# Pairing input rows to shorten the even-frequency DFT matmuls, and loading channel 128 in 16 rows in place of 8, in a fused FFT and cosine-gated layer kernel

## The chip, the cores and the metric

The kernel runs on one core of a Trainium2 chip. The metric is the time on the device in microseconds (us), as the median of several executions. The profile's "span" is the time from the first to the last instruction of one profiled execution; it is about 2 us shorter than the device time of the same execution.

A NeuronCore has several engines that run their own instruction streams and wait for each other through semaphores. In the profile they are called PE (matrix multiply, with PEld for its weight loads), DVE (vector), ACT (scalar and activation functions), POOL (a second elementwise engine, slower here: 1.00 us for a 128x381 add, where DVE takes 0.95 us for 128x762; it also issues gathers) and SP (here it only issues DMA transfers; "SPq" lines are these issues). In this kernel data from DRAM comes by DMA, and channel 128 is also moved across partitions by DMA.

## The reference, cut to what matters

```python
def _attn_ref(x):                       # x: (8, 3008, 256) float32
    X = np.fft.fft(x, axis=1)           # along the 3008 rows
    X = np.fft.fft(X, axis=2)           # along the 256 channels
    return X.real.astype(np.float32)

def _moe_ref(x, w_in, w_out):           # x: (24064, 256), w_in: 256 x 2048, w_out: 2048 x 256
    h = x @ w_in
    g = h * np.cos(h)
    return (g @ w_out).astype(np.float32)
```

The output is the second function applied to the first, with the batch and row axes merged. Everything is float32.

## The kernel before

The channel transform is multiplied into `w_in` once, at the start, so only the row transform (a DFT of length 3008) is left to do per batch. It is done as matmuls with constant cosine and sine matrices.

Symmetry keeps these small. Rows `s`, `1504-s`, `1504+s` and `3008-s` are first added and subtracted ("folds"), so only rows 0 to 752 are left as the contraction. Each batch then has four transforms: real and imaginary part, each for even and odd frequencies `k`. Even `k` has 377 output columns (`NE`) and odd `k` 376 (`NO`).

The 753 rows lie as 128 partitions by six "slots" `m`. In every transform the even rows contribute to columns `k` and their mirror alike, so their matmuls need only half the columns (four matmuls of `NH` = 189, the "first part", then unfolded by DVE). The odd rows fill three slots, which need all 377 columns each (the "second part"). In the kernel before:

```python
NH = 189

def _row_of(m):                       # slot m, partition p -> row
    p = np.arange(128)
    return 4 * p + m if m < 4 else 512 + 2 * p + m - 4

def dft_parts(ri, kodd, par):
    mats = MC[ri, kodd]
    if par:                           # second part: odd rows, slots 1, 3, 5
        n = NO if kodd else NE
        for t in range(3):
            c = AW + t * NE
            yield 2 * t + 1, 0, mats[:, c : c + n]
    else:                             # first part: even rows
        for t, m in enumerate((0, 4, 2, 4)):
            yield m, t // 2 * NH, mats[:, t * NH : (t + 1) * NH]
```

Rows are loaded by plain DMA where they ascend with the partition (`L[0]` and `L[3]`). The mirrored ones come by indirect DMA ("gather"), issued by POOL, since they descend: four gathers per batch.

```python
GATHERS = [(2, 0), (2, 1), (1, 0), (1, 1)]
...
eng = nc.gpsimd if b == 1 else nc.sync        # plain loads: batch 1 on POOL's queue
for j, row in ((0, 0), (3, HALF)):
    pin(eng.dma_start(out=L[j][:, 0 : 4 * ND], in_=xrows(b, row, 4, 128, 4)))
    pin(eng.dma_start(out=L[j][:, 4 * ND :], in_=xrows(b, row + 512, 2, 128, 2)))
```

Channel 128 is handled apart, because the 129 distinct channels don't fit on 128 partitions. `load_ext` picks that one channel out of `x` (4-byte elements, a whole row apart in DRAM). `turn_ext` stores it to DRAM (`xe_dr`) and reads it back with rows on partitions (`xs`). `fold_ext`, on POOL, folds it; `dft_ext`, on PE, transforms it.

```python
def turn_ext():
    rows, xs = state["rows"], state["xs"]
    for j in range(4):
        spin(out=xe_dr[j], in_=rows[j][:, 0:768])             # spin = DMA issued by SP
    for j in range(4):
        spin(out=xs[:, j, :, 0:4], in_=xe_dr[j][:, 0:512].rearrange("b (p m) -> p b m", m=4))
        spin(out=xs[:, j, :, 4:6], in_=xe_dr[j][:, 512:768].rearrange("b (p m) -> p b m", m=2))
```

All engines' work is placed in one static schedule. `at(t, fn)` places the emission of `fn` at a nominal time. It fixes the order of the instructions on each engine, not the time at which they run. One "step" (nominal `T` = 4.8 us) handles 256 columns of the result, and there are 376 steps.

```python
e0 = 12 * T
at(e0 + 1.35, fold_ext)                   # POOL
at(e0 + 4.75, dft_ext)                    # PE
...
for b in range(1, NB):
    s0 = (b - 1) * steps_b                # steps_b = 47
    l0 = s0 - (8 if b > 1 else 0.5)       # loads and gathers, from step l0
    f0 = max(7, s0 - 1)                   # folds on POOL, from step f0 to f1
    f1 = s0 + 38
    ...                                   # DFTs: even k at s0+28 and s0+34, odd k at s0+38 and s0+42
```

## Time and profile before

| | before |
|---|---|
| device time, median of 3 | 1956.05 us (1955.8 to 1957.27) |
| profiled span, mean granted PE clock | 1954.1 us, 0.999 |
| PE busy | 1936.6 us, 99% |
| one step (11 matmuls of 256 columns) | 4.75 us |

The first part of the page gives each engine's busy time, its share of the span and its count of instructions. The fourth part gives the shares of the chain of waits, followed back from the last instruction. The kernel before:

```profile
span 1954.1 us, 28165 instructions
PE 1936.6 (99%) x8858; PEld 1650.5 (84%) x8858; DVE 1418.9 (73%) x2354; ACT 1453.6 (74%) x2791; POOL 1357.7 (69%) x1869
...
PE 92%; DVE 3%; ACT 1%; issue 1%; POOL 1%; DVEq 0%; POOLq 0%
```

PE is the limit: it idles 17.5 us out of 1954. A change can win only by giving PE less to do, and it loses by making PE wait.

The timeline view has one line per run of equal instructions: start in us, duration in us, engine, source line, operation, output and inputs, shapes, count and, in brackets, idle time before it and what ended it. PE in one even transform of the kernel before, its first part and its second part:

```profile
182.53 1.45 PE L266 MATMUL H<-MC,e 128*128 128x189 f32 x8
...
193.32 2.07 PE L266 MATMUL H<-MC,e 128*128 128x377 f32 x6
```

(Each matmul instruction appears as two records.) The second line is what the change shortens. The two times include some overlap at the ends, so that group costs PE 1.9 us up to the next one (at 195.23 us).

The start, on DVE and PE; "e" is the even fold, "pA" the first DFT, "H<-Rr,Wc" the first matmul of the main loop's step 0:

```profile
18.75 0.17 DVE L352 COPY e<-xl 128x6 f32<-128x6 f32 x1
```

```profile
21.82 1.55 PE L266 MATMUL pA<-MC,e 128*128 128x189 f32 x8 [0.77 <-DVE e L331]
...
31.57 1.02 PE L266 MATMUL H<-Rr,Wc 128*128 128x256 f32 x4
```

And channel 128: the DMA issues on SP, then POOL's fold of it ("xs", "xe").

```profile
24.09 52.95 SPq L168 DMA_DIRECT2D x<-in_x_dram  x5
77.16 13.87 SPq L168 DMA_DIRECT2D xe_dr<-x  x4
91.08 6.32 SPq L168 DMA_DIRECT2D xs<-xe_dr  x8
```

```profile
98.96 1.00 POOL L331 TENSOR_TENSOR e<-xl 128x381 f32<-128x381 f32 x1
99.91 0.39 POOL L275 TENSOR_TENSOR xs<-xs 128x96 f32<-128x96 f32 x1
```

The loads occupy SP's queue for 53 us, and POOL reaches its fold at 99.91 us without a wait.

### The profile page before, as it was taken

To read this page: it belongs to the slowest core of one execution; us is meant where nothing else is said; L and a number is where in the kernel's file an instruction comes from. 1 tells how busy PE (TensorE), PEld (TensorE's weight loads), DVE (VectorE), ACT (ScalarE), POOL (GpSimd) and SP (SyncE) were. 2 spreads that over 40 slices of the span, in tenths; PEclk is the share of its full clock that TensorE was granted. 3 is DMA by queue.
4 is the path that set the end of the run, shared out by engine and by line. 5 is a ranking of instruction groups with operands and counts; after the bars stand their busy time and mean duration, and the time that the engine had idled before them with its cause. 6 is when DMAs were issued, how large, how long until landed. Compare 5 with 4: busy or idle time off the path is not lost.

```text
span 1954.1 us, 28165 instructions
## 1 busy us (share of the span) xinstructions
PE 1936.6 (99%) x8858; PEld 1650.5 (84%) x8858; DVE 1418.9 (73%) x2354; ACT 1453.6 (74%) x2791; POOL 1357.7 (69%) x1869
## 2 busy tenths in 40 slices
PE   9999999999999999999999999999999999999998
PEld 4878888888888888888888888888888888888887
DVE  5777677777777767777677777777767777677777
ACT  3777777777777777777777777777777777777775
POOL 5977667776677766777677776777657776555654
PEclk9999999999999999999999999999999999999999
DMA  9720210102111020110301003011030100000101
GB/s 301 6 39 9 65 33 20 26 9 68 28 20 21 9 83 17 21 20 9 87 19 18 16 9 87 11 27 20 9 82 12 30 19 10 14 11 15 19 12 22
DMA packets 260161, 66.16 MB, mean 34 GB/s; under 512 B 247283, under 2 KB 250107, under 8 KB 260012
## 3 DMA queue, kind: packets, MB, share of 16 engines
q1 hardware_dynamic: 253292, 49.93, 13.8%
q0 software_dynamic: 4544, 14.17, 2.3%
q8 instruction: 70, 1.15, 0.2%
q14 instruction: 79, 0.65, 0.1%
q10 hardware_dynamic: 2176, 0.26, 0.1%
HBM read 39.48 MB, written 24.79 MB: 33 GB/s over the span
## 4 chain that ended last, share of the span: by engine, by line
PE 92%; DVE 3%; ACT 1%; issue 1%; POOL 1%; DVEq 0%; POOLq 0%
PE H L266 37%; PE pB L266 16%; PE pC L266 16%; PE pD L266 16%; PE pA L266 8%; DVE G L723 1%; ACT G L278 1%; POOL G L275 1%; DVE v L272 0%; DVE G L272 0%; DVE M L272 0%; ACT E L278 0%; DVE ab L272 0%; DVE u L272 0%; DVE ot L831 0%
## 5 line engine op out<-in xcount | busy, mean ns | idle before, releaser
L275 POOL TENSOR_TENSOR G<-G 128x256 f32<-128x256 f32 x1500 | 1079.2, 730 | 560.0 <-DVE G L723 467.8
L723 DVE SCALAR_TENSOR_TENSOR G<-H,G 128x512 f32<-128x512 f32 x376 | 257.0, 684 | 266.4 <-ACT G L278 266.4
L272 DVE TENSOR_TENSOR G<-H,G 128x512 f32<-128x512 f32 x376 | 260.0, 692 | 220.8 <-ACT G L278 217.8
L278 ACT ACTIVATE G<-H 128x512 int32<-128x512 f32 x376 | 224.6, 597 | 233.3 <-DVE G L272 231.9
L266 PE MATMUL pC<-G,WT 128*128 128x256 f32 x1504 | 387.4, 379 | 2.3 <-DVE u L272 1.9
L266 PE MATMUL H<-Ir,Ws 127*128 127x256 f32 x1504 | 387.5, 379 | 0.7 <-ACT E L278 0.7
L266 PE MATMUL H<-Rr,Wc 128*128 128x256 f32 x1504 | 387.2, 380 | 1.0 <-ACT H L278 0.8
L278 ACT ACTIVATE H<-Rb,wex 128x256 f32<-128x256 f32 x752 | 360.2, 479 | 25.9 <-DVE G L723 10.7
L278 ACT ACTIVATE E<-H 128x512 f32<-128x512 f32 x376 | 224.3, 596 | 200.7 <-PE H L266 198.0
L266 PEld LDWEIGHTS H<-Rr,Wc 128*128 128x128 f32 x1504 | 283.6, 190 | 49.1 <-ACT H L278 3.3
L266 PEld LDWEIGHTS pC<-G,WT 128*128 128x128 f32 x1504 | 283.8, 189 | 46.5 <-PE H L266 6.4
L266 PEld LDWEIGHTS H<-Ir,Ws 127*128 127x128 f32 x1504 | 282.3, 189 | 45.0 <-ACT E L278 6.1
L278 ACT ACTIVATE G<-G,halfpi 128x512 f32<-128x512 f32 x376 | 269.5, 717 | 1.5 <-DVE G L272 1.5
L272 DVE TENSOR_TENSOR M<-G,M 128x512 f32<-128x512 f32 x376 | 257.7, 685 | 0.0
L272 DVE TENSOR_TENSOR G<-E,H 128x512 f32<-128x512 f32 x376 | 255.3, 679 | 1.8 <-issue 1.7
L723 DVE SCALAR_TENSOR_TENSOR G<-G,M 128x512 f32<-128x512 f32 x376 | 254.2, 676 | 0.4 <-ACT M L278 0.3
L278 ACT ACTIVATE M<-M,halfpi 128x512 f32<-128x512 f32 x376 | 246.4, 655 | 0.4 <-DVE M L272 0.3
L266 PE MATMUL pB<-G,WT 128*128 128x256 f32 x752 | 227.4, 384 | 1.0 <-POOL G L275 0.8
L278 ACT ACTIVATE M<-G 128x512 int32<-128x512 f32 x376 | 224.1, 596 | 0.0
L266 PE MATMUL pB<-G,w 128*128 128x256 f32 x752 | 223.7, 379 | 0.1
L266 PE MATMUL pA<-G,w 128*128 128x256 f32 x752 | 223.8, 379 | 0.0
L266 PE MATMUL pD<-G,WT 128*128 128x256 f32 x752 | 223.8, 379 | 0.0
(134 smaller groups left out, 1793.6 us busy)
## 6 DMA issues: line engine op xcount, KB each, us to landing
out_dram<-ot SPq DMA_DIRECT2D x496, 32.0 KB
xl<-in_x_dram SPq DMA_DIRECT2D x14, 512.0 KB
out_dram<-ot SPq DMA_DIRECT2D x256, 2.0 KB
MC<-dft_mats SPq DMA_DIRECT2D x4, 943.5 KB
Rb<-r SPq DMA_DIRECT2D x10, 376.0 KB
xl<-in_x_dram SPq DMA_DIRECT2D x14, 256.0 KB
w<-in_moe_w_in_dram SPq DMA_DIRECT2D x4, 512.0 KB
w<-in_moe_w_out_dram SPq DMA_DIRECT2D x1, 2048.0 KB
```

Source lines behind the costliest of these rows:

```text
L266: nc.tensor.matmul(out_, lhsT=lhsT, rhs=rhs, start=start, stop=stop, skip_group_check=True)
L272: pin(nc.vector.tensor_tensor(out=o, in0=a, in1=b, op=op))
L275: pin(nc.gpsimd.tensor_tensor(out=o, in0=a, in1=b, op=op))
L278: pin(nc.scalar.activation(out=o, in_=i, func=func, **kw))
L723: nc.vector.scalar_tensor_tensor(out=o, in0=h, scalar=TWO_PI, in1=c, op0=ALU.mult, op1=ALU.mult)
```

## The change

For even `k`, rows `s` and `752-s` have equal cosines and sines up to a sign that depends on the parity of `k/2`. If both lie on one partition, they can be summed and differenced first; half of the columns need only the sum, and half only the difference. So two slots of odd rows at 377 columns each become one sum at 189 columns and one difference at 188: three 377-column passes become two. The price is a new layout. Slot D1 holds rows `247-2p`, which descend with the partition, so more slots must be gathered (4 gathers per batch become 10). The even columns come out sorted by parity, so writes into the ring are strided and split in two. Channel 128 follows the same layout and is loaded with 16 (half, batch) rows outermost in place of 8 batches. The core of the diff:

```diff
-NH = 189
+NK = 189
+NH = (190, 189)
+C0, D1, C2, Y, M1, X1 = range(6)
 def _row_of(m):
-    return 4 * p + m if m < 4 else 512 + 2 * p + m - 4
+    return (4 * p, 247 - 2 * p, 4 * p + 2, 504 + 2 * p, 505 + 2 * p, 249 + 2 * p)[m]
 ...
-    GATHERS = [(2, 0), (2, 1), (1, 0), (1, 1)]
+    GATHERS = [(0, (D1, D1 + 1)), (3, (D1, D1 + 1))] + [
+        (j, part) for j in (2, 1) for part in ((5, 6), (3, 4), (1, 3), (0, 1))
+    ] + [(1, (4, 5))]                                   # the last one in the last batch only
 ...
-        eng = nc.gpsimd if b == 1 else nc.sync          # 4 plain loads per batch
+        pin(nc.sync.dma_start(out=out, in_=in_))        # 8 plain loads per batch, all on SP
 ...
+        def pair(key, s, width, first, second):         # sum -> pf, difference -> slot M1
+            d, m = (s[:, n * width : (n + 1) * width] for n in (D1, M1))
+            tt(pf[:, 0:width], d, m, first)
+            tt(m, d, m, second)
 ...
     def dft_parts(ri, kodd, par):
+        if kodd:
+            parts = ((D1, 0, NO), (X1, 0, NO), (M1, 0, NO))
+        else:
+            parts = ((6, 0, NK), (M1, NK, NE - NK), (X1, 0, NE))    # 6 = the sum tile pf
 ...
     def turn_ext():
-            for j in range(4):
-                spin(out=xe_dr[j], in_=rows[j][:, 0:768])
+            for g in range(2):
+                spin(out=xe_dr[g], in_=rows[g][:, 0:768])
+                spin(out=xr_dr[g], in_=rows[g][:, 247::-1])         # reversed, to DRAM
 ...
+                spin(
+                    out=xs[0:124, g, :, 7:8],
+                    in_=xr_dr[g].rearrange("b (p m) -> p b m", m=2)[:, :, 0:1],
+                )
 ...
-    fold_now("z1 z3 c0 e0 o0 c3 e3 c2 e2 E2 x1 c1 e1 E0 EO0")       # batch 0, on DVE
+    fold_now("z1 z3 c0 e0 o0 c3 e3 c2 e2 E2 x1 c1 e1 E0 EO0 P0")
-        l0 = s0 - (8 if b > 1 else 0.5)
+        l0 = s0 - (8 if b > 1 else 1.2)
```

`in_=rows[g][:, 247::-1]` is a store to DRAM that reads its source backwards, one float at a time.

## The prediction

> **What bounds it.** TensorE: the page gives PE 99% busy (1936.6 of 1954.1 us), the chain of waits is 92% PE, and PE's waits sum to about 10 us. A plain step (eleven 256-column matmuls) repeats every 4.75 us in the timeline; DVE, ACT and POOL work in its shadow. Clock 0.999.
>
> **What is removed.** In the timeline three 377-column matmuls take 1.90 us from first start to the next group: 1.68 ns a column (256 columns: 0.433 us). Even k now streams 189+188+377 = 754 columns instead of 1131, and 4x190 instead of 4x189: 373 columns, 0.62 us less per even transform. Batches 1 to 7: 14 x 0.62 = 8.7 us. The channel-128 transform: perhaps 0.2 us. Batch 0's three even transforms (1.9 us of PE) lie in the start, where PE waits for DVE; I count nothing there.
>
> **What is added.**
> 1. POOL: gathers per batch go from 4 to 10 (0.97 us each, about 1.1 us with issue). The sums take 3.03 us per 4.75 us step, a fold 1.0 (1.15 with its copy). A gather alone fits; gather plus fold (5.1 to 5.3 us) doesn't. By the instruction order they meet in three steps per batch (four in the last). Before, POOL's idle there after the fold is 0.2, 0.7, 0.6 us, so it falls about 1.7 us behind; the third sum is finished about 0.9 us before PE loads weights from it. Estimate: PE loses 0.8 us per batch from batch 2 on, about 4.5 us in all, as "PE pB <- POOL G". The pair sums (two of about 0.46 us) have steps of their own: free.
> 2. DVE/ACT: strided ring writes split each 377-column write in two (DVE 0.54 becomes about 0.68 us, ACT 0.48 about 0.65): free from batch 1 on.
> 3. Start: DVE is busy without a gap from 18.5 to 30 us and the first main matmul (31.6 us) waits for it. P0, P2, two tiny adds and split writes add about 1.2 us. Ten gathers at 1.27 us end at 15 us and land at 18 to 19, when the fold that needs the last of them ran (18.8). About 1.3 us lost.
> 4. Channel 128: 53 us of issue on SP (24,576 elements). The Trainium skill, "DMA: Bandwidth & Descriptors", section "Why a DMA increments its semaphore by 16 and not by 1", says a copy uses the largest count up to 16 that divides the slowest dimension: 8 before, 16 now. I expect about 27 us. Batch 1's loads follow on the same queue and arrive near 58 us, before folds at 75. But reversed copies add small elements, and 124 partitions give 4 engines; POOL's fold of it (at 100 us) may wait: 1 us expected, at most 5.
>
> **Sum.** -8.9 +4.5 +1.3 +1 = -2, and I lean to less POOL loss: **1952 us**, range 1945 to 1958. Faster by over 2%: 0.5%; within 2%: 98.5%; slower by over 2%: 1%.
>
> **What would show it.** PE busy down about 10 us. PE waits for POOL G at three steps per batch, total 3 to 6 us (before 0.8). First main matmul at 32 to 34 us. The SP issue of channel 128 about halved. POOL busy up about 55 us.
>
> **What would make it wrong.** POOL's slack larger (then 1946); the channel-128 fold or batch-1 loads late, stalling POOL for many us (1960); strided PSUM or SBUF access costing DVE much more.

## The result, and the profile after

| | before | after |
|---|---|---|
| device time, median of 4 runs each | 1956.36 us (1955.8 to 1957.27) | 1985.84 us (1984.26 to 1989.48) |
| ratio | | 1.0153 (95%: 1.0135 to 1.017) |
| profiled span, granted PE clock | 1954.1 us, 0.999 | 1982.3 us, 0.992 |

A ratio here is the mean time of one kernel's fast runs over that of the other's fast runs of the same rounds, so it is not quite the ratio of the medians. The changed kernel is 1.5% slower. That is within 2%, as the prediction's likeliest class had it, but 1985.84 us lies far outside its range of 1945 to 1958, and on the wrong side of zero.

The page of the changed kernel: its busy times, two rows of its 40-slice table (busy tenths of PE, then the granted clock in tenths), and the chain of waits.

```profile
span 1982.3 us, 28384 instructions
PE 1932.9 (98%) x8858; PEld 1649.2 (83%) x8858; DVE 1425.2 (72%) x2386; ACT 1454.8 (73%) x2807; POOL 1418.9 (72%) x1947
...
PE   7959999999999999999999999999999999999998
...
PEclk9979999999999999999999999999999999999999
...
PE 84%; DVE 5%; POOL 4%; ACT 3%; issue 2%; SPq 1%; DMA 1%; DVEq 0%; POOLq 0%
```

PE is busy less than before (1932.9 us against 1936.6), as the change wants. But PE idles 49 us in place of 17.5. The table says where: a slice is 49.6 us, and apart from the last slice, which ran out in the kernel before as well, PE is below 9 tenths only in the first and the third. In the third the granted clock also drops. The view of waits names the wait, as engine, tile, who is waited for, total us, number and longest:

```profile
PE H L276 <- POOL xe L285: 23.7, 1, 23.7
PE pA L276 <- DVE e L341: 2.6, 1, 2.6
PE pB L276 <- POOL G L285: 2.3, 8, 0.6
```

One wait of 23.7 us, for POOL's fold of channel 128, is most of the loss of 28. POOL itself was waiting, as its timeline shows:

```profile
104.17 1.00 POOL L341 TENSOR_TENSOR e<-xl 128x381 f32<-128x381 f32 x1
129.22 0.59 POOL L285 TENSOR_TENSOR xs<-xs 128x64 f32<-128x64 f32 x2 [24.05 <-DMA out_dram<-ot]
```

The bracket blames a DMA "out_dram<-ot", the store of results. That label is an inference from semaphore events, and the instruction doesn't read `ot`; it reads `xs`. The DMA records agree: the last 4-byte packet of the reads into `xs` ended at 128.95 us, 0.27 us before POOL went on. What SP was doing until then shows why. Its timeline in the changed kernel:

```profile
25.13 27.06 SPq L162 DMA_DIRECT2D x<-in_x_dram  x3
52.33 14.81 SPq L182 DMA_DIRECT2D xl<-in_x_dram  x8
67.20 0.42 SPq L162 DMA_DIRECT2D xe_dr<-x  x1
67.66 0.65 SPq L162 DMA_DIRECT2D xr_dr<-x  x1
68.36 6.57 SPq L162 DMA_DIRECT2D xe_dr<-x  x1
74.97 1.93 SPq L162 DMA_DIRECT2D xr_dr<-x  x1
77.01 39.34 SPq L162 DMA_DIRECT2D xs<-xe_dr  x3
```

The issue time of the loads was indeed halved, 52.95 us to 27.06, and the first store was issued 10 us earlier than before. Then the first three reads of `xs` take 39 us to issue, where all eight took 6.32 us before. They follow the two reversed stores to `xr_dr`.

PE did not simply lose those 24 us. It came back to a slow clock:

```profile
130.26 3.73 PE L276 MATMUL H<-MC,xe 128*8 128x190 f32 x28 [23.66 <-POOL xe L285]
```

In the kernel before, the same 28 records took 2.09 us:

```profile
101.32 2.09 PE L266 MATMUL H<-MC,xe 128*8 128x189 f32 x28
```

The wait of 23.7 us and these 1.6 us make 25.3 us together. In the view by windows (window and its length, busy us and instructions of PE, PEld, DVE, ACT and POOL, granted clock, DMA share, GB/s) the clock shows directly:

```profile
110.00:115.00 5.00, 0.00 (x0) 0.00 (x0) 0.00 (x0) 0.00 (x0) 0.00 (x0) 0.50 0.26 5
...
130.00:135.00 5.00, 4.74 (x33) 2.64 (x34) 0.00 (x0) 0.00 (x0) 4.63 (x9) 0.68 0.32 51
```

During the stall the granted clock was 0.50, and 0.68 in the window from 130 to 135 us, in which PE resumes. The clock records behind this view have it at 0.50 from 109.30 us, 2.7 us after PE's last matmul, to 133.19 us. The Trainium skill, "TensorE: Matmul & The Clock Gate", section "Why this matters for your kernels", asks for no PE idle gap above about 3 us, since such a gap brings the gate back to half rate. This trace agrees: a gap of 23.7 us, and a clock of 0.50.

### A ledger by steps

Every step of the main loop begins with the same matmul, "H<-Rr,Wc". Its start in one trace minus its start in the other, over the 376 steps, is a running account of who is ahead. From the two traces (us; a positive number means that the changed kernel is late):

```
step   what lies there                                change of the offset    offset
0      start of the main loop                            +4.30                  4.30
1-12   end of the start                                  +0.9                   5.21
13     channel-128 fold                                  +25.4                 30.58
17-29  folds of batch 1, on POOL                         +1.2                  31.75
s0+31, s0+37 in batches 1-7: 14 even transforms          -0.50 to -0.63 each, -8.6 in all
s0+2 to s0+4 in batches 2-7: gathers beside folds        +0.8 to +1.0 each, +5.2 in all
others (small steps)                                     +0.5
after step 319                                           -0.7
end                                                                            28.2
```

So the change did win what it was made for, 8.6 us. It lost 25.4 us once, 5.2 us at the start, and 6.4 us in POOL's gathers and folds.

The gain and its mechanism are visible in the transform. The first even transform of batch 1 in the changed kernel, its second part:

```profile
225.08 0.48 PE L276 MATMUL H<-MC,pf 128*128 128x189 f32 x2
225.40 1.12 PE L276 MATMUL H<-MC,e 128*128 128x188 f32 x4
```

The 128x189 pass on the sum ("pf") and the passes on the other two slots take the place of the six records of 377 columns above. (The second line groups the 188-column difference with the 377-column slot, under the first one's shape.) Up to the next matmul, at 226.35 us, they cost 1.27 us, where the old group cost 1.9.

At the start, DVE waits for a gather, and PE for DVE:

```profile
21.37 0.17 DVE L362 COPY e<-xl 128x6 f32<-128x6 f32 x1 [3.81 <-DMA xl<-in_x_dram,ix]
```

```profile
24.43 2.90 PE L276 MATMUL pA<-MC,e 128*128 128x190 f32 x8 [2.59 <-DVE e L341]
...
35.87 1.13 PE L276 MATMUL H<-Rr,Wc 128*128 128x256 f32 x4 [0.26 <-issue]
```

DVE gets to this copy 2.6 us later than before (18.75). From there to the end of the unfold that frees bank pA for PE's next transform it takes 11.3 us in place of 9.5, so it adds 1.9 us of work: the pair sums, the small sums for channel 128, and the split unfold. That transform is then 0.2 us shorter on PE, and 2.6 + 1.9 - 0.2 = 4.3 us is what step 0 is late. (The pA group also takes 2.90 us in place of 1.55, at a granted clock of 0.50, which lasted from 23.97 to 27.38 us. That costs nothing: PE is idle again later, for 1.55 us from 31.3 us, until DVE has freed pA at 32.7 us.)

### The profile page after: what moved, and what is told of

It is laid out like the page before. It is cut to its first block, busy times and chain, and to the rows that moved or that the text cites. A ratio compares the mean times of both kernels' runs of the same rounds, so it can differ in the third digit from the quotient of the medians.

```text
span 1982.3 us, 28384 instructions
## 1 busy us (share of the span) xinstructions
PE 1932.9 (98%) x8858; PEld 1649.2 (83%) x8858; DVE 1425.2 (72%) x2386; ACT 1454.8 (73%) x2807; POOL 1418.9 (72%) x1947
## 4 chain that ended last, share of the span: by engine, by line
PE 84%; DVE 5%; POOL 4%; ACT 3%; issue 2%; SPq 1%; DMA 1%; DVEq 0%; POOLq 0%
PE H L276 33%; PE pB L276 14%; PE pC L276 14%; PE pD L276 14%; PE pA L276 7%; POOL G L285 2%; DVE G L790 2%; ACT G L288 1%; SPq L162 1%; POOL xl L152 1%; DVE G L282 1%; POOL e L341 1%; DVE v L282 1%; DVE M L282 1%; ACT E L288 1%
## 5 line engine op out<-in xcount | busy, mean ns | idle before, releaser
L276 PE MATMUL pD<-G,w 128*128 128x256 f32 x752 | 223.7, 379 | 0.0
```

The source lines that it names most:

```text
L276: nc.tensor.matmul(out_, lhsT=lhsT, rhs=rhs, start=start, stop=stop, skip_group_check=True)
```

## The experiments

The main theory was that the reversed stores of channel 128 to DRAM (4-byte elements) drain so slowly that every later transfer of the chain is late. Its rivals were the new place of batch 1's loads, which now stand ahead of the channel-128 stores on SP's queue, and the two reads of 124 partitions (E3). All edits are against the changed kernel. "Jump" is what the offset to the kernel before gains between step 12 and step 13; in the changed kernel it is 25.4 us. E1 to E4 ran together on one chip, E5 to E7 on a second, E8 and E9 on a third.

### E1: reverse on ScalarE, store contiguously

```diff
-                spin(out=xr_dr[g], in_=rows[g][:, 247::-1])
+    def reverse_ext():
+        act(x1[0 : 4 * NB, 768:1016], x1[0 : 4 * NB, 247::-1])     # one ACT copy
+        for g in range(2):
+            spin(out=xr_dr[g], in_=rows[g][:, 768:1016])
+        ...                                                        # then the xs reads, as they were
+    at(7 * T + 1.46, reverse_ext)
```

> The change, but the reversal of channel 128's rows is done by one ScalarE copy in SBUF and the store to the scratch tensor is then a plain one of contiguous rows. Theory R (the reversed store, 7936 elements of 4 bytes, is the stall: it held the queue from about 71 to 109 us): the copies behind it end near 97 us, the channel-128 fold on POOL no longer waits 24 us, PE's 23.7 us wait vanishes, about 1960 us. Rival Q (batch 1's plain loads, moved to the SP queue ahead of it, are the delay): little change, 1980 us or more.

Measured: correct, 1960.04 us (1958.71 to 1961.37, 2 runs) against 1956.59 us before; ratio 1.0016 (0.9987 to 1.0045). The jump is 0.07 us, and the 23.7 us wait is gone. The reversal is one ACT instruction, and the reads that follow now issue without delay:

```profile
78.67 0.39 ACT L289 ACTIVATE x<-x 32x248 f32<-32x248 f32 x1
```

```profile
79.09 0.77 SPq L163 DMA_DIRECT2D xr_dr<-x  x2
79.97 2.99 SPq L163 DMA_DIRECT2D xs<-xe_dr  x3
```

A 0.39 us instruction in an idle spot of ACT buys back 25 us. The batch-1 loads and the 124-partition reads are still as in the changed kernel, so neither of them makes the stall by itself. Since E1 changes the element size as well as the timing of the chain, the next three runs hold the rivals against each other.

### E2: batch 1's plain loads back on POOL's queue

```diff
+        eng = nc.gpsimd if b == 1 else nc.sync
         def load(out, in_):
-            pin(nc.sync.dma_start(out=out, in_=in_))
+            pin(eng.dma_start(out=out, in_=in_))
```

> The change, but batch 1's eight plain loads are issued by POOL again, as before, so they don't stand ahead of channel 128's copies on the SP queue. Theory Q: the stall goes, about 1960 to 1965 us. Theory R: the copies only start some 6 us earlier, the stall shrinks from 24 to about 18 us, about 1980 us.

Measured: correct, 1987.98 us (1986.97 to 1988.99, 2 runs), ratio 1.0159 (1.0129 to 1.0188). The reads of `xs` hang just as long, and PE's wait stays:

```profile
77.26 40.10 SPq L162 DMA_DIRECT2D xs<-xe_dr  x3
```

```profile
PE H L278 <- POOL xe L287: 20.6, 1, 20.6
```

The jump is 23.0 us, and it is smaller only because PE arrives 4.7 us later: POOL's fold starts at 130.89 us, 1.7 us later than in the changed kernel (129.22). Without the loads ahead of them, the reversed stores were issued no earlier (69.27 and 75.87 us, against 67.66 and 74.97), so the order of SP's queue is not the cause. The move even costs 4.6 us elsewhere, between steps 1 and 6: POOL spends the time until 50.2 us on issuing gathers and these eight loads, and PE then waits 3.6 us for its sums. That the change moved these loads to SP was right.

### E3: the 124-partition reads in two pieces, 112 and 12

```diff
-                spin(
-                    out=xs[0:124, g, :, 7:8],
-                    in_=xr_dr[g].rearrange("b (p m) -> p b m", m=2)[:, :, 0:1],
-                )
+                for p0, p1 in ((0, 112), (112, 124)):
+                    spin(
+                        out=xs[p0:p1, g, :, 7:8],
+                        in_=xr_dr[g].rearrange("b (p m) -> p b m", m=2)[p0:p1, :, 0:1],
+                    )
```

> The change, but the two 124-partition copies of channel 128 are cut into 112 + 12 partitions[...]. If the 4-engine copies carry the stall (theory F): about 1962 us. Theory R: they are two times 6 us of a chain of 60, so 8 to 10 us of the stall go, about 1976 us.

Measured: correct, 1983.54 us (1982.88 to 1984.2, 2 runs), ratio 1.0136 (1.0107 to 1.0166). The jump is 21.6 us, against 25.4:

```profile
PE H L276 <- POOL xe L285: 19.6, 1, 19.6
```

The 8 to 10 us that were expected did not come: the jump is 3.8 us smaller. Part of that is the start of this run, which was 1.5 us later, so that PE had less to wait. POOL's fold starts 2.5 us earlier than in the changed kernel (126.67 us against 129.22), though the first read of `xs` moved 2.3 us later (105.64 against 103.35). The 124-partition reads are thus a small part, some 2 to 5 us; one trace of each doesn't settle it closer, since the time from the first read to the fold also differs among runs with unsplit reads (25.9 us in the changed kernel, 23.4 in E8). The Trainium skill, "DMA: Bandwidth & Descriptors", section "Why a DMA increments its semaphore by 16 and not by 1", says that the number of engines is the largest one up to 16 that divides the slowest dimension of both sides. That gives 4 engines for 124 partitions, and 16 and 12 for the two pieces. The gain agrees in direction, and so does the halved issue of the loads (8 batches to 16 rows, 52.95 to 27.06 us); no view here counts the engines.

### E4: the same reversed store, its elements 64 bytes apart in DRAM

```diff
-    xr_dr = dpool.tile([2, 2 * NB, 248], FP, tag="xr", name="xr_dr")
+    xr_dr = dpool.tile([2, 2 * NB, 248 * 16], FP, tag="xr", name="xr_dr")
-                spin(out=xr_dr[g], in_=rows[g][:, 247::-1])
+                spin(out=xr_dr[g][:, ::16], in_=rows[g][:, 247::-1])
-                    in_=xr_dr[g].rearrange("b (p m) -> p b m", m=2)[:, :, 0:1],
+                    in_=xr_dr[g].rearrange("b (p m) -> p b m", m=32)[:, :, 0:1],
```

> The change, but the reversed store puts its 4-byte elements 64 bytes apart in the scratch tensor, with as many elements, still reversed; the copies that read it follow. If neighbouring 4-byte writes to DRAM get in each other's way, the store takes under 10 us instead of 38 and the stall goes: about 1960 us. If a 4-byte element costs this much wherever it lands, or reading SBUF backwards does: as the change, about 1985 us.

Measured: correct, 1959.37 us (1959.32 to 1959.41, 2 runs), ratio 1.0013 (0.9984 to 1.0042). The jump is 0.07 us. The number of elements, their size and their reversed order are all as in the changed kernel; only the distance between their destinations differs. And yet the stall is gone:

```profile
77.72 11.93 SPq L162 DMA_DIRECT2D xs<-xe_dr  x3
```

So neither "many 4-byte elements" nor a reversed source suffices as the cause. What costs the time is 4-byte elements written side by side in DRAM. (The two reads of that tensor take spaced elements too, but they come after the store, whose own time the DMA records under E8 and E9 give.)

### E5: E1, and a fold order at the start that works while the last gather is on its way

```diff
-    fold_now("z1 z3 c0 e0 o0 c3 e3 c2 e2 E2 x1 c1 e1 E0 EO0 P0")
+    fold_now("z1 z3 c0 e0 o0 c3 e3 c2 e2 E2 o3 o2 O2 x1 c1 e1 E0 EO0 P0")
     ...
-    fold_now("o1 O0 o3 o2")
+    fold_now("o1 O0")
     ...
-    fold_now("O2 EO2 P2")
+    fold_now("EO2 P2")
```

> E1 (ScalarE reversal) with VectorE's first folds in another order: o3, o2, O2, which need no late gather, run before e1 instead of after it, where VectorE stood idle 2.5 to 3.8 us for the last of ten gathers. If the later start (first main matmul 4.2 to 4.8 us after that of the kernel before) comes from the late gathers plus VectorE's added work: 2 to 2.7 us of it go, about 1957.5 us. If it comes from PE or from the clock after its idle time: no change, 1960 us.

Measured: correct, 1956.18 us (1956.08 to 1958.16, 4 runs) against 1957.0 us before (11 runs), ratio 0.9992 (0.9966 to 1.0018). Step 0 is 1.69 us later than in the kernel before, in place of 4.30 (changed kernel) and 4.84 (E1); step 1 is 2.53 us late. What is left at step 0, 1.7 us, is the 1.9 us of work that the change adds on DVE there, less the 0.2 us that PE saves. So the start's loss was two things, a delay of 2.6 us by a late gather, which another order hides, and extra DVE work, which it doesn't.

### E6: E1, and the folds of each batch begin three steps later

```diff
-        f0 = max(7, s0 - 1)
+        f0 = max(7, s0 + 2)
```

> E1 with each later batch's folds begun three steps later, so that no POOL step holds both a gather and a fold. Theory P (gather plus fold overfill a 4.75 us step, and PE loses 0.8 to 0.9 us in each of batches 2 to 7, seen as steps of the offset between the kernels): the six offset steps go, 5 us, about 1955 us. If they come from DVE or from the DMA traffic of the gathers: they stay, about 1960 us.

Measured: correct, 1956.14 us (1954.02 to 1957.42, 4 runs), ratio 0.9985 (0.9959 to 1.0012). This moves the first folds of batches 2 to 7 behind their last gather. In the offsets, all six jumps are gone:

```
offset to the kernel before (us), first step of each batch's stretch and five steps on
step            47     52      94     99      141    146     188    193     235    240     282    287
changed       30.50  31.13   29.53  30.38   29.59  30.50   29.24  30.03   29.50  30.38   29.09  30.11
E1             4.85   5.45    3.88   4.74    4.01   4.90    3.66   4.45    3.98   4.84    3.58   4.57
E6             7.21   7.20    5.59   5.59    4.79   4.79    3.53   3.52    2.98   2.98    1.68   1.74
```

E6 started 2.4 us worse than E1 (step 1 late by 7.16 us against 4.80), with the same code up to there; E3's start was worse too (6.70), so the start varies from run to run. Within the trace, E6 gains 5.3 us on E1 from step 40 to the end (-2.97 at the end, +2.36 at step 40), which matches the 5.2 us of the ledger. In the middle of the kernel that is one cause, shown by its removal: POOL has room for a gather or for a fold in a step, not for both.

The collision itself, in the changed kernel on POOL (batch 5): a gather, a fold's copy, a fold and four sums in one step take 5.1 us, in a step of 4.75.

```profile
1020.96 0.97 POOL L152 DMA_INDIRECT xl<-in_x_dram,ix  x1
1021.93 0.21 POOL L362 COPY e<-xl 128x6 f32<-128x6 f32 x1
1022.08 1.00 POOL L341 TENSOR_TENSOR e<-xl 128x381 f32<-128x381 f32 x1
1023.04 3.02 POOL L285 TENSOR_TENSOR G<-G 128x256 f32<-128x256 f32 x4
```

### E7: all four mends together

E1, E3, E5 and E6, and the folds of batch 1 shifted by 0.4 of a step so that its 34 pieces double up in other steps of the 31 that it has:

```diff
-                int(f0 + n * (f1 - f0) / n_big) * T + 1.3,
+                int(f0 + 0.4 * (b == 1) + n * (f1 - f0) / n_big) * T + 1.3,
```

> E1, E3, E5 and E6 together, and batch 1's folds shifted so that none of its three doubled steps stands at a combination step. If the parts add up: -25.4 (stall) -2.5 (start) -5 (gathers) -0.8 (batch 1) against the change, about 1951 to 1952 us, faster than the kernel before by 0.2 to 0.3%; what then remains against it is 14 x 0.62 us won less 2 to 3 us lost at the start.

Measured: correct, 1951.44 us (1950.58 to 1952.77, 6 runs) against 1957.0 us before (1955.91 to 1965.76, 11 runs), ratio 0.9965 (0.9945 to 0.9985). Three of the eleven runs of the kernel before were near 1965.5; without them its mean is 1956.56 us, the mean of E7 is 1951.60 us, and the ratio would be 0.9975. So the honest size is about 5 us, a quarter of a per cent. E7 beats both kernels.

```profile
span 1948.4 us, 28382 instructions
PE 1926.6 (99%) x8858; PEld 1648.0 (85%) x8858; DVE 1423.2 (73%) x2386; ACT 1454.9 (75%) x2808; POOL 1417.2 (73%) x1947
```

PE is busy 10.0 us less than before. Its trace ends 5.69 us before that of the kernel before: step 1 is 2.16 us late, step 29 3.07 us, and the rest is mostly the gain of the even transforms. The shifted folds cut the jump at step 19 from 0.83 to 0.13 us, but a new one of 0.77 us stands at step 13 (0.07 in E1 and E5). One of the doubled steps now lies just before channel 128's fold:

```profile
96.11 1.96 POOL L342 TENSOR_TENSOR e<-xl 128x381 f32<-128x381 f32 x2
```

POOL then has no gap until 108.2 us, and PE gets its sums and channel 128's fold late (the transform of that channel takes PE 2.52 us in place of 2.16 in E5). So the shift mostly moved this loss: from step 1 to step 29 E7 loses 0.91 us, where E5 loses 1.26. In its start DVE has the odd folds to do where it used to wait:

```profile
17.43 1.80 DVE L342 TENSOR_TENSOR o<-xl 128x762 f32<-128x762 f32 x2
...
21.04 0.17 DVE L363 COPY e<-xl 128x6 f32<-128x6 f32 x1 [0.63 <-DVE xl L369]
```

### E8 and E9: is it the direction or the distance?

E8 writes the same packed destination from a source read forward. It picks the wrong rows, so its result is wrong (relative error 1.064). E9 keeps the reversal and puts the elements 16 bytes apart.

```diff
 E8
-                spin(out=xr_dr[g], in_=rows[g][:, 247::-1])
+                spin(out=xr_dr[g], in_=rows[g][:, 0:496:2])
 E9
-                spin(out=xr_dr[g], in_=rows[g][:, 247::-1])
+                spin(out=xr_dr[g][:, ::4], in_=rows[g][:, 247::-1])
```

> The change, but the store to the scratch tensor reads its row forwards, every second element, and writes 4-byte elements next to each other, as many as before (the values for 124 rows of channel 128 are wrong on purpose, so the result is wrong). If packed neighbouring 4-byte writes are what is slow: the stall stays, about 1980 to 1986 us. If the backward order is: it goes, about 1960 us.

> E4 with the elements 16 bytes apart instead of 64. If only direct neighbours disturb each other: as E4, about 1960 us. If all writes to one block of 64 bytes do: four share one, where sixteen did, so the store takes some 10 to 20 us, its chain ends between 97 and 115 us, and the stall is 0 to 10 us, 1960 to 1970 us.

Measured: each one run, of unknown state, on a chip on which the one run of the kernel before took 1966.95 us. E8 took 1983.4 us, E9 1974.02 us (correct). Those times are not compared with the others here; the waits inside the profiles are. POOL's wait in front of the fold, E8 and then E9 (the DMA label is the same misattribution as above):

```profile
POOL xs L285 <- DMA out_dram<-ot: 22.4, 1, 22.4
```

```profile
POOL xs L285 <- DMA out_dram<-ot: 14.0, 1, 14.0
```

E9's wait is above the 0 to 10 us that were expected: four elements to 64 bytes already cost more than half of the stall. The DMA records of the traces line up over the four kernels with such a store. Taken are the 4-byte packets on SP's queue from the issue of the first store of the chain to the first 16-byte read of `xs` (7,974 to 8,077 in each; the two stores have 7,936 elements). E1, which has no such store, is added for comparison:

| kernel | elements in DRAM | source | mean time of a 4-byte packet | 99% of them begun by | first read of xs moves at | jump at step 13 |
|---|---|---|---|---|---|---|
| changed | 4 B apart | reversed | 83 ns | 102.2 us | 103.35 us | 25.4 us |
| E8 | 4 B apart | forward | 85 ns | 102.9 us | 104.1 us | 24.3 us |
| E9 | 16 B apart | reversed | 62 ns | 93.9 us | 95.5 us | 15.4 us |
| E4 | 64 B apart | reversed | 17 ns | 84.5 us | 86.1 us | 0.1 us |
| E1 | contiguous rows | reversed by ACT | no such store | | 81.0 us | 0.1 us |

The mean is carried by a minority of long packets: in the changed kernel the median is still 9 ns, but one packet in twenty took over 440 ns. In all four, the first read of `xs` moves within 2 us of the end of the store's elements. In the three that stall, another 23 to 26 us go by from that read to POOL's fold, so the stall follows from that time. Direction makes no difference (changed kernel against E8). Distance decides.

### What follows from the experiments

The stall of 25.4 us comes from 7,936 four-byte elements being written side by side in DRAM; once that has made the chain late, the reads of 124 partitions in one piece add a few us of it. E1, E4, E8 and E9 show the first from four sides. Of the rivals, one fell (E2) and one shrank to a small part (E3), which costs nothing when the chain is early (E1, E4).

What stays open: why neighbouring 4-byte writes to DRAM disturb each other. No run shows the mechanism. Open too are the variation of the start from run to run (step 1 late by 4.8 to 7.2 us with the same code there), the runs near 1965 us of the kernel before, and the 1.7 us of DVE work at the start, which no run tried to hide. Moving channel 128's fold to a later step was not run.

## Why the prediction was wrong, point by point

- **What bounds it: right.** PE was 99% busy before, and the losses above are waits of PE, and its half clock after the longest one.
- **What is removed: right.** 0.62 us per even transform and 8.7 us in all were predicted; the fourteen steps show 0.50 to 0.63 us each, 8.6 us in all. "PE busy down about 10 us" showed as only 3.7 us in the changed kernel. About 3 us of the rest are two groups of matmuls at half clock (3.73 us in place of 2.09, and 2.90 in place of 1.55); E5, whose clock stays at full until the end, shows 6.9 us, and E7 10.0 us. What makes up those last 3 us was not traced. The 0.2 us hoped for from channel 128's transform did not come: 2.16 us in E1 against 2.09.
- **Item 1, POOL: right in mechanism and size.** 4.5 us were predicted, 0.8 per batch from batch 2 on; 5.2 us were measured, 0.8 to 1.0 per batch, and E6 removes all of it. The sign that was named ("PE pB <- POOL G", 3 to 6 us) shows only 2.3 us (0.8 before); more of the lateness appears at PE's weight loads, where "PEld pB <- POOL G" rose from 11.7 to 18.5 us. One row of the view need not hold the whole of a wait. What the item missed are the folds of batch 1, which has 34 pieces for 31 steps and lost 1.2 us.
- **Item 2, strided writes on DVE and ACT: right.** They cost next to nothing from batch 1 on: no step outside the named ones added as much as 0.5 us, and all of these together added 0.5.
- **Item 3, the start: right in mechanism, too small.** 1.3 us were predicted, and step 1 was 5.1 us late. Two terms were mis-sized. The last packets of the gathers ended at 20.5 us and not at 18 to 19, and DVE came to their fold at 21.37 us, 2.6 us late, where the prediction had nearly none. The extra DVE work was 1.9 us, not 1.2. E5 separates the two. So the first main matmul came at 35.87 us and not at 32 to 34.
- **Item 4, channel 128: this is the step that failed.** "POOL's fold of it (at 100 us) may wait: 1 us expected, at most 5" was 25.4 us. The halving of the load was right (52.95 to 27.06 us). The risk was even named ("reversed copies add small elements, and 124 partitions give 4 engines"), so the wait was in the sum, but not the cost that makes it: the prediction prices the channel's loads from the trace, and has no number for the reversed 4-byte stores behind them. In the changed kernel the 4-byte packets that read that channel took 17 ns in the mean, and those that write it packed took 83 ns; the store held back the reads behind it until 103 us. Whether the prediction had the cost of a read in mind for the stores, its text doesn't say.
- **"What would make it wrong": named, too small.** "The channel-128 fold [...] late, stalling POOL for many us (1960)" is what happened, and then PE's clock fell as well, which no term had. With the stall taken out and nothing else (E1), the time is 1960.04 us, still 2 us above the range, by the start that item 3 had too small; with the mends of E7, 1951.44 us, where the prediction had 1952. That agreement is partly luck, since E7 also removes the losses that the prediction had counted.

The margin should have been the warning. In the kernel before, the last read of channel 128 was issued only 2.5 us ahead of its fold. A chain with so little slack, onto which the diff puts a kind of transfer that the trace has never shown, can't be given "at most 5".

## What to carry to other kernels

Before crediting a change with a smaller main term, list every transfer that it adds whose kind (element size, direction, neighbours in DRAM) the old trace doesn't show, and follow it to the first instruction that needs it; cost it from the same kind of transfer, or widen the range by the slack that it can eat. If data has to be reversed or permuted within a partition, let an engine with idle time do it in on-chip memory (here 0.39 us on ACT) and keep DRAM stores contiguous; if elements have to be scattered to DRAM one by one, keep them apart (64 bytes removed the stall here, 16 did not). And when a static schedule gives a side engine more pieces, move them to steps where it has room (E6), since an engine at 72% busy can still be full in the very step that counts.

## What the Trainium skill lacked or had wrong

- "DMA: Bandwidth & Descriptors", section "Rules for kernel authors", says that a strided last dimension "Lowers to one descriptor per element" and should be made contiguous. The trace agrees (about 8,000 packets of 4 bytes for the 7,936 elements of the two reversed stores). The page has overheads per packet for small descriptors, but no cost of such a packet that depends on how close its neighbours lie. Here: 83 to 85 ns a packet for writes 4 bytes apart, 62 ns at 16 bytes, 17 ns at 64 bytes, and 17 ns for the 4-byte reads of a channel (25 ns in the kernel before), whose elements lie a whole row apart in DRAM (all means). It also doesn't say that reversing a unit-stride source falls under this rule; it does.
- The same page, section "Specifications", gives 512 B as the least size for line rate and says that below it the transfer does a read-modify-write. It doesn't say that the distance between small neighbouring writes matters. Elements of 4 bytes at a distance of 64 bytes are also far below 512 B, and took a fifth of the time of packed ones (17 ns against 83). The stated mechanism could fit if it concerned only neighbours within some unit; no run here shows that.
- "TensorE: Matmul & The Clock Gate", section "Why this matters for your kernels": its limit of about 3 us of idle agrees with the clock of 0.50 in the stall. It is no sharp limit here: a wait of 2.31 us at the start of E9 and one of 2.59 us in the changed kernel stood beside a clock of 0.50, and one of 2.98 us in E8 stood beside a full clock. What decides between them was not tested.
